# Score steps of four blocks instead of two or three, in an attention and long-convolution kernel

## The chip, the cores and the metric

The kernel runs on one core of a Trainium2 chip. The core has five engines, each with its own instruction queue, that meet only in semaphores: TensorE (PE, matmuls, with its weight loads PEld), VectorE (DVE), ScalarE (ACT), GpSimd (POOL) and SyncE (SP); the last two mostly start DMAs here. Matmuls write to PSUM, which has eight banks of 128 partitions x 512 fp32. The metric is the device time of one execution in microseconds (us), the median over runs.

## The reference

Two independent computations write the two halves of the output.

```python
# A: multi-head attention, S = 2048, D = 512, 32 heads of 16
qkv = (x @ wqkv) split into q, k, v by head
p = softmax(q k^T * 16**-0.5)          # 32 x 2048 x 2048
a = (p @ v, heads joined) @ wo
# B: gated long convolution, 512 channels
kv = (4-tap causal filter of k, by channel) * v
y  = causal convolution of kv with ssm_k along S, by channel   (there by FFT)
b  = q * (y + kv * ssm_D)
out = concatenate([a, b])
```

The 32 x 2048 x 2048 exponentials of A are the largest item: 2048 blocks of 128 keys x 512 queries.

## The kernel before

**Blocks and groups.** A *group* is one of 32: four heads (of the eight that share 128 rows of a projection, every second) and 512 queries. It has 64 *blocks*, 16 key tiles of 128 times 4 heads, and the head of a block decides which 32 rows of the PE array its score matmul takes (`tile_position=(32 * s, 0)`); matmuls in different row groups run side by side. The blocks go through in order in a queue, in *steps* T = 0, 1, 2, ...

**A step.** `emit_qk` takes the step's PSUM banks and as many blocks, `qk_mm` issues their scores (L803). One block of a step may go to VectorE, the others are made into exponentials by one ScalarE instruction over neighbouring banks (`emit_exp`, L836) that writes the ring PT (17 blocks). On VectorE a block takes four operations (`exp_on_dve`): the first reads the bank (L882), and three work in SBUF on the ring PTD (8 blocks): L888, L892, L896. They give two halves, both of which are multiplied by V. `emit_pv` multiplies exponentials by V (L933), four heads side by side in four column groups, into bank 6 (PVB), over the whole group; two steps after the scores at the earliest. When a group is complete, `finish_group` transposes bank 6 on VectorE (L1007) and normalises (L1014, L1018, and for every second group L1027).

**Banks.** Banks 0 to 5 are for scores; even steps take them from the left, odd ones from the right, up to `MOST` = 3 a step, so that a step's banks are read while the next step's are written. `take_banks` moves the border as banks come free and may let the last bank come late (`late`). Bank 7 (BGB) collects the convolution.

**Background work on TensorE.** *Units* are the projections q, k, v, the 4-tap filter kv, the output projection op and the transposes of a finished piece of convolution ("turn"). Ahead of step `N_OPEN` = 64 they use bank 7. Later each needs a *window*: `hold` takes one score bank out of circulation for `LEN` = 3 steps, and `unit_step` puts units into it in halves. In the meantime no block goes to VectorE where a unit is close. The convolution (`conv_lags`, L1143) runs in bank 7 in portions between the other work. `warm_up` fills gaps with matmuls on zeros (L1353).

**What sets the order.** All orders are written out when the program is built. A planner (`Eng.op`) keeps a running time for each engine, adds a duration to each operation, and the rules (`room`, `unit_step`, `advance`, `pv_step`) decide by these times what to issue next. VectorE's later operations stand in `flow` and are let in by `advance`; `urgent` puts an operation in at once. Each engine then runs its list in order, with semaphore waits. For every 256 words of TensorE's code three DMA loads of filter rows (`feed_wr`) are released.

**The end.** The last 2 x `N_TAIL` = 18 blocks go in nine steps of two, without VectorE, while the output projection of the last queries fills in.

Of the kernel before, what the change touches and what calls it, by code (L numbers as in the profile page):

```python
# [34 lines left out]
R_PT = 17  # L35
# [5 lines left out]
N_OPEN = 64  # L41
KV1 = 3
LAGS = 8
PACE = 1.2
# [16 lines left out]
N_TAIL = 9  # L61
N_LAST = 0
# [3 lines left out]
R_PTD = 8  # L66
T_DVE = 6
SLOT = 18
OPEN = 80
CLOSE = 10  # L70
REST = 4
LEN = 3
WIN_D = 2
# [4 lines left out]
PLAN = 710  # L78
JOIN = 0.1
JOIN2 = 0.15  # L80
MOST = 3
Q_DUE = 24
LOOK = 8
GAP = 7
TAIL_GAP = 0
AHEAD = 6
KZ_LATE = 8.0
KEEP = 4
BACKLOG = 6.0
# [7 lines left out]
TURN = 0.05  # L97
SOON = 0.5
NEAR = 0.1
FULL = 1.6  # L100
BUSY = 0.85
FILL_GAP = 0.2
RATE = 4.2
CAP = 18.0
WAIT = 3
# [147 lines left out]
def bass_concat_heads__mha_block__ssm_conv_h3__prompt_kernel(  # L253
# [47 lines left out]
    DR = sb("DR", [128, NQB * NG, 16], FP32)  # L301
# [175 lines left out]
    def pe_unit(u, bank, parts=(0, 1, 2, 3)):  # L477
# [3 lines left out]
        if kind == "q":  # L481
# [3 lines left out]
            def mm(e, dc):  # L485
                return e.matmul(PS[:, bank, :], lhsT=WQ[:, dc, o * 128:(o + 1) * 128], rhs=xT[:, dc, qb * 512:(qb + 1) * 512],  # L486
                                start=(dc == 0), stop=(dc == 3))
        elif kind == "k":
# [5 lines left out]
            def mm(e, dc):  # L494
                return e.matmul(PS[:, bank, c0:512], lhsT=WK[:, dc, o * 128:(o + 1) * 128],  # L495
                                rhs=xT[:, dc, sc * 512 + c0:(sc + 1) * 512], start=(dc == 0), stop=(dc == 3))
        elif kind == "kv":
# [5 lines left out]
            def mm(e, b):  # L503
                ins = None
                for m in range(4):
                    c0 = LEFT + 128 * (4 * i + 3 - b) - m
                    ins = e.matmul(PS[:, bank, 128 * b:128 * b + 128], lhsT=KTR[kt_i][:, kt_c, c0:c0 + 128], rhs=DG[:, c, m, :],
                                   start=(m == 0), stop=(m == 3))
                return ins
        else:  # L510
# [10 lines left out]

        def fn(e):
            ins = None
            for j in parts:
                ins = mm(e, j)
            return ins
        return pe.op(fn, deps, run=mm_run * len(parts), kind="F")
# [133 lines left out]
    ends = [4, 4]  # L661
    LAST_BLKS = 2 * N_TAIL + 3 * N_LAST
    NL = NQB * NG - 1
    held = {}
    win = {}
    queue = list(range(NBLK))

    def take_banks(T):
        if len(queue) == LAST_BLKS:
            end[0] = T + N_TAIL + N_LAST  # L670
        if len(queue) <= LAST_BLKS:
            return [3 * (T % 2) + i for i in range(2 + (len(queue) > 2 * N_TAIL))]
        start = max(pe.t, at(h_exp.get(T - 2)) + 0.13)
        late["bank"] = None

        def comes_free(b):
            if held.get(b) == "w" and (part[0] or T <= win["stop"] and (T < win["begin"] + 2 or near(T, CLOSE))):
                return False
            if at(bank_free[b]) + 0.13 > start + JOIN and late["bank"] is None and T >= 2:
                if at(bank_free[b]) + 0.13 + JOIN2 <= at(h_exp[T - 1]) - 0.36:  # L680
                    late["bank"] = b
            return at(bank_free[b]) + 0.13 <= start + JOIN or late["bank"] == b

        def give(b):
            if held.pop(b, None) == "w":
                win.clear()
                win["last"] = T
        if T % 2 == 0:
            while ends[0] < min(ends[1], MOST) and comes_free(ends[0]):
                give(ends[0])  # L690
                ends[0] += 1
            banks = list(range(ends[0]))
        else:
            while ends[1] > max(ends[0], 6 - MOST) and comes_free(ends[1] - 1):
                give(ends[1] - 1)
                ends[1] -= 1
            banks = list(range(ends[1], 6))
        if T >= N_OPEN and near(T, OPEN) and T >= win.get("last", 0) + REST and "bank" not in win and len(banks) > 2 and late["bank"] is None and len(queue) > LAST_BLKS + OPEN_LAST:
            b = hold(T, banks, "w")
            win.clear()  # L700
            win.update(bank=b, begin=T, stop=T + LEN)
        return banks

    def near(T, most):
        job = next_unit(T)
        return job is not None and job[0] - T <= most

    def hold(T, banks, kind):
        if T % 2 == 0:
            b = banks.pop()  # L710
            ends[0] -= 1
        else:
            b = banks.pop(0)
            ends[1] += 1
        held[b] = kind
        h_held[b] = T
        return b

    end = [10 ** 6]
    h_held = {}  # L720
    late = {"bank": None}
# [28 lines left out]
    h_blk = {}  # L750
    def emit_qk(T):
        banks = take_banks(T)
        n = min(len(banks), len(queue) - LAST_BLKS) if len(queue) > LAST_BLKS else len(banks)
        bl = next_blocks(n)
        extra = dve_block(T, bl) if late["bank"] is None else None
        d_bank = hold(T, banks, "d") if extra is not None else None
        if extra is not None:
            if extra not in bl:
                bl.pop()
                bl.append(extra)  # L760
            n -= 1
        banks = banks[:n]
        for b in bl:
            queue.remove(b)
        banks_of[T] = banks
        chunks[T] = bl
        for b in bl:
            chunk_of[b] = T
        on = list(zip(bl, banks + [d_bank]))
        if late["bank"] in banks and len(queue) >= LAST_BLKS:  # L770
            i = banks.index(late["bank"])
            h = qk_mm(on[:i] + on[i + 1:])
            emit_exp(T, bl, banks, h, extra, d_bank, [on[i]])
        else:
            h = qk_mm(on)
            emit_exp(T, bl, banks, h, extra, d_bank, [])

    def next_blocks(n):
        bl = []
        for b in [b for b in queue[:LOOK] if blk_group(b) == blk_group(queue[0])] + queue[:n]:  # L780
            if len(bl) < n and b not in bl and (blk(b)[2] not in [blk(x)[2] for x in bl] or len(bl) + 1 > 4):
                bl.append(b)
        for b in queue[:n]:
            if len(bl) < n and b not in bl:
                bl.append(b)
        return bl
# [30 lines left out]
    def emit_exp(T, bl, banks, h, extra, d_bank, more):  # L817
        n = len(banks)
        if extra is not None:
            on_dve[extra] = len(on_dve)  # L820
            exp_on_dve(extra, d_bank, h)
# [4 lines left out]
        for i, b in enumerate(bl[:n]):  # L826
            assert p0 + i not in pt_used
            pt_used[p0 + i] = b
            pt_of[b] = p0 + i
        if more:  # L830
            if at(bank_free[more[0][1]]) + 0.13 > pe.t + 0.1:
                advance(pe.t)
                pv_step(T)
            h = qk_mm(more)
        free = max([pt_free[p] for p in range(p0, p0 + n) if p in pt_free], key=lambda d: d[1], default=None)
        h_exp[T] = act.op(lambda e: e.activation(PT[:, p0:p0 + n, :].rearrange("p b f -> p (b f)"),  # L836
                                                 PS[:, banks[0]:banks[0] + n, :].rearrange("p b f -> p (b f)"),
                                                 ACT.Exp, scale=EXP_SCALE, bias=EXP_BIAS),
                          [h, free], us=(0.065 + 0.4257 * n, 0.205 + 0.4257 * n))
        for b, bank in zip(bl[:n], banks):  # L840
            bank_free[bank] = h_blk[b] = h_exp[T]
# [8 lines left out]
    def dve_block(T, bl):  # L850
        if len(bl) < 3 or WIN_D and "bank" in win and (part[0] or WIN_D > 1 and near(T, CLOSE)) or T < T_DVE or len(queue) < LAST_BLKS + 3 * (TAIL_GAP - N_LAST) + 3:
            return None
        i = len(on_dve)
        if i >= R_PTD and i - R_PTD not in h_ptd:
            return None
        todo = sum(us[0] for f in flow for _, _, _, us, _ in f)
        if max(dve.t - pe.t, 0.0) + todo > BACKLOG:
            return None
        n, j = sub(bl[-1])
        left = len([b for b in queue if sub(b) == (n, j)])  # L860
        if left - 3 >= 2.6 * GAP:
            return bl[-1]
        if n == NL:
            if (n, j + 1) not in [sub(b) for b in queue]:
                return None
            ahead = [b for b in queue if sub(b) == (n, j + 1)]
        else:
            n += 1
            ahead = [b for b in queue if blk_group(b) == n]
            if len(ahead) < 4 * KT - AHEAD + 1 or n not in h_q or (OF[n], 0) not in h_k:  # L870
                return None
        rows = [blk(b)[2] for b in bl[:-1]]
        return next((b for b in ahead[:4] if blk(b)[2] not in rows), ahead[0])
# [84 lines left out]

    acts, dves = [], []
# [6 lines left out]
    def pv_step(T):  # L966
# [519 lines left out]
```

## Time and profile before

| | before |
|---|---|
| median of 3 runs | 784.3 us (781.27 to 792.7) |
| the profiled execution | 787.65 us, its span 785.9 us |
| granted TensorE clock, mean | 0.978 |
| ScalarE busy | 754.8 us |
| TensorE busy | 736.5 us |
| VectorE busy | 686.0 us |
| GpSimd busy | 90.7 us |

All rows and views are of one profiled execution; its time is 3.35 us over the median. A row of the grouping view names line, engine, operation, what is written and read, the shape and the count, then busy time and mean length of one (ns), then the idle time ahead of these instructions and what ended it. A row of the timeline has the start, the length, and in brackets the idle time of the engine before it with what ended it. Instructions of an engine overlap a little, so their lengths add up to more than the busy time, and the time that one takes in a chain is read from starts.

### The profile page before, as it was taken

The numbers are of one execution on the slowest core, as the hardware profiler recorded it, in microseconds if no ns is written. First come the engines' busy times: TensorE is split into PE (matmuls) and PEld (weight loads), VectorE is DVE, ScalarE is ACT, GpSimd is POOL, SyncE is SP. The second block draws the span as 40 slices with busy tenths as digits, with TensorE's granted clock in tenths as the row PEclk, the third lists the DMA queues.
The fourth block names the chain that finished last, engine by engine and source line by source line (L and its number), as shares of the span: only waits on it lengthen the run. The fifth ranks groups of instructions, "written<-read, shape, count | busy, mean of one in ns | idle before, by whom it ended". The sixth has DMA issues, their size and how long they took to land.

```text
span 785.9 us, 31776 instructions
## 1 busy us (share of the span) xinstructions
PE 736.5 (94%) x14087; PEld 319.2 (41%) x14132; DVE 686.0 (87%) x1887; ACT 754.8 (96%) x735; POOL 90.7 (12%) x160
## 2 busy tenths in 40 slices
PE   8999998998989999999999999999999999999987
PEld 3233443443424344344443334443443434434453
DVE  4999777899989999898798889989999978889992
ACT  6999999999979999999999999999999999999994
POOL 6300102200400201000022020004011010000000
PEclk9999999999979999999999999999999999999995
DMA  9895149858546576667865766857686775767510
GB/s 221 217 287 175 36 155 238 288 168 266 175 169 217 195 235 210 220 231 212 260 201 181 233 210 215 258 185 245 211 275 185 222 250 178 256 236 224 193 57 28
DMA packets 88888, 161.45 MB, mean 205 GB/s; under 512 B 50256, under 2 KB 53968, under 8 KB 88368
## 3 DMA queue, kind: packets, MB, share of 16 engines
q1 hardware_dynamic: 81760, 150.43, 60.7%
q0 software_dynamic: 5792, 8.66, 3.6%
q8 instruction: 112, 1.84, 1.0%
q10 hardware_dynamic: 1200, 0.33, 0.2%
q14 instruction: 24, 0.20, 0.1%
HBM read 142.61 MB, written 6.42 MB: 190 GB/s over the span
## 4 chain that ended last, share of the span: by engine, by line
ACT 60%; DVE 22%; PE 17%; issue 1%; DMA 1%
ACT PT L836 60%; DVE PTD L882 9%; PE PS L803 6%; PE PS L933 5%; DVE PTD L892 4%; DVE PTD L888 3%; DVE PTD L896 2%; PE PS L1143 2%; PE PS L1081 2%; DVE DT L1007 1%; DMA xT<-in_A_x_dram 1%; PE PS L486 1%; DVE QN L1176 1%; DVE KTo L543 0%; DVE VA L571 0%
## 5 line engine op out<-in xcount | busy, mean ns | idle before, releaser
L836 ACT ACTIVATE PT<-PS 128x1024 bf16<-128x1024 f32 (+2 forms) x731 | 752.6, 1251 | 19.3 <-PE PS L803 18.0
L803 PE MATMUL PS<-QT,KTo 32*128 32x512 bf16 (+2 forms) x2248 | 292.5, 370 | 22.6 <-ACT PT L836 9.5
L882 DVE TENSOR_SCALAR PTD<-PS 128x512 uint16<-128x512 f32 x406 | 276.1, 684 | 35.6 <-PE PS L803 34.3
L933 PE MATMUL PS<-PT,VA 128*32 128x512 bf16 (+2 forms) x1800 | 207.2, 377 | 11.8 <-DVE DT L1007 7.5
L1143 PE MATMUL PS<-WR,KV 128*28 128x128 bf16 (+8 forms) x8192 | 199.4, 220 | 0.0
L1143 PEld LDWEIGHTS PS<-WR,KV 128*28 128x28 bf16 (+7 forms) x8192 | 143.9, 95 | 63.9 <-issue 34.4
L892 DVE TENSOR_TENSOR PTD<-PTD 128x512 f16<-128x512 f16 x406 | 163.4, 417 | 1.3
L803 PEld LDWEIGHTS PS<-QT,KTo 32*128 32x128 bf16 x2248 | 76.1, 92 | 206.0 <-ACT PT L836 150.2
L933 PE MATMUL PS<-PTD,VA 128*32 128x512 f16 (+1 forms) x896 | 149.2, 370 | 1.2 <-DVE PTD L896 1.2
L896 DVE TENSOR_SCALAR PTD<-PTD 128x512 uint16<-128x512 uint16 x406 | 111.0, 286 | 0.9
L888 DVE TENSOR_SCALAR PTD<-PTD 128x512 uint16<-128x512 uint16 x406 | 109.7, 290 | 1.3
L348 POOL DMA_DIRECT2D QT<-QS x120 | 61.0, 516 | 414.7 <-DVE QS L534 369.0
L933 PEld LDWEIGHTS PS<-PT,VA 128*32 128x32 bf16 x1800 | 52.8, 95 | 124.5 <-issue 90.2
L1353 PE MATMUL PS<-IDN,ZW 128*32 128x512 bf16 (+3 forms) x197 | 51.6, 317 | 0.1
L933 PEld LDWEIGHTS PS<-PTD,VA 128*32 128x32 bf16 x896 | 37.3, 96 | 5.6 <-DVE PTD L896 1.7
L1007 DVE STREAM_TRANSPOSE DT<-PS 128x512 f32<-128x512 f32 x31 | 22.1, 713 | 5.9 <-PE PS L933 5.3
L1089 DVE CAST OUTA<-PS 128x512 bf16<-128x512 f32 x15 | 10.3, 687 | 12.5 <-PE PS L1081 12.2
L348 POOL DMA_DIRECT2D out_dram<-OUTA x15 | 8.7, 582 | 108.0 <-DVE OUTA L1089 34.1
L1353 PEld LDWEIGHTS PS<-IDN,ZW 128*32 128x32 bf16 x197 | 16.3, 97 | 11.1 <-issue 5.8
L1081 PE MATMUL PS<-WKV,OTN 128*128 128x512 bf16 (+1 forms) x54 | 18.8, 422 | 2.1 <-issue 0.8
L543 DVE CAST KTo<-PS 128x512 bf16<-128x512 f32 (+1 forms) x16 | 10.7, 670 | 10.1 <-PE PS L495 10.1
L518 PE MATMUL PS<-WKV,xT 128*128 128x128 bf16 x256 | 19.3, 220 | 0.0
(71 smaller groups left out, 232.7 us busy)
## 6 DMA issues: line engine op xcount, KB each, us to landing
WR<-kz_scratch SPq DMA_DIRECT2D x256, 512.0 KB, 5.9
KV<-KV SPq DMA_DIRECT2D x16, 256.0 KB, 5.4
kz_scratch<-WR SPq DMA_DIRECT2D x1, 2176.0 KB, 9.4
QN<-in_B_q_dram POOLq DMA_DIRECT2D x2, 1024.0 KB, 10.1
out_dram<-QN POOLq DMA_DIRECT2D x2, 1024.0 KB, 6.5
QT<-QS POOLq DMA_DIRECT2D x120, 16.0 KB, 3.5
out_dram<-OUTA POOLq DMA_DIRECT2D x15, 128.0 KB, 2.9
QN<-in_B_ssm_k_dram SPq DMA_DIRECT2D x1, 1024.0 KB, 8.5
```

The lines of the kernel that those rows point to most:

```text
L348: f(outp, inp).then_inc(dsem.sem, 16)
L803: ins = e.matmul(PS[:, bank, i * w:i * w + w], lhsT=KTo[32 * s:32 * s + 32, OF[n_] % 2, kt * 128:(kt + 1) * 128], rhs=QT[32 * s:32 * s + 3 ...
L836: h_exp[T] = act.op(lambda e: e.activation(PT[:, p0:p0 + n, :].rearrange("p b f -> p (b f)"), PS[:, banks[0]:banks[0] + n, :].rearrange("p ...
L882: h_f = urgent(lambda e: e.tensor_scalar(fix_u, PS[:, bank, :], FIX_ADD, FIX_HI, ALU.add, ALU.min), [h, h_ptd.get(i - R_PTD)], slack=S_FX)
L888: st["h"] = dve.op(lambda e: e.tensor_scalar(mant_u, fix_u, MANT, HALF_BITS, ALU.bitwise_and, ALU.bitwise_or), [st["h"]], us=us)
L892: st["h"] = dve.op(lambda e: e.tensor_tensor(mant, fix, mant, ALU.mult), [st["h"]], us=us)
L896: lambda e: e.tensor_scalar(fix_u, fix_u, OCTAVE, ONE_MORE, ALU.bitwise_and, ALU.bitwise_or), [st["h"]], us=us)
L933: ins = e.matmul(dst, lhsT=w, rhs=rhs, start=first, stop=last, tile_position=(0, 32 * s))
L1007: h_t = urgent(lambda e: e.transpose(out=dt, in_=PS[:, PVB, :]), [h, h_mul.get(n - 1)], slack=S_T, us=(0.63, 0.751))
L1081: ins = e.matmul(PS[:, b, c0:c1], lhsT=OTN[:, PAIRS.index((o, qb)), t * 128:(t + 1) * 128], rhs=WO[:, o, c0:c1], start=(o == 0), stop=(o = ...
L1143: ins = e.matmul(PS[32 * g:32 * g + 2 * ((30 - d) // 2 + 1), BGB, 128 * kk:128 * kk + w], lhsT=kv, rhs=WR[:, r + g, S - 64 * d - 128:S - 6 ...
L1353: pe.op(lambda e, s=s, k=k, rhs=rhs, bank=bank, rows=rows, c0=c0, first=first: e.matmul(PS[32 * s:32 * s + rows, bank, c0:c0 + 128 * k], l ...
```

## The change

Steps have four blocks, with one block in each row group. Bank 4 and the pair 0-1 or 2-3 (in turns) go to ScalarE in two instructions, first one block, then two; bank 5 goes to VectorE. Where VectorE gets no block, ScalarE does two pairs, (4, 5) and then (0, 1) or (2, 3). So banks 4 and 5 are used by every step. Windows are gone: units use bank 7 between pieces of the convolution, in quarters, and q, k and op matmuls of 128 columns are cut into four of 32 columns in four column groups (`columns`), as P times V has them.

```diff
-R_PT = 17
+R_PT = 15
...
-N_OPEN = 64
...
+N_OPEN = 50
...
-N_TAIL = 9
...
+N_TAIL = 10
...
-R_PTD = 8
...
+R_PTD = 10
+DV_MIN = 4
+LOOK = 16
+LAST_PV = 5
...
-BACKLOG = 6.0
+BACKLOG = 4.0
...
-    DR = sb("DR", [128, NQB * NG, 16], FP32)
+    DR = sb("DR", [128, 2, 16], FP32)
...
+    def columns(e, dst, w, rhs, **kw):
+        ins = None
+        for g in range(0, 128, 32):
+            ins = e.matmul(dst[g:g + 32], lhsT=w[:, g:g + 32], rhs=rhs, tile_position=(0, g), **kw)
+        return ins
...
+            return [2 * (T % 2) + i for i in range(2)]
+        return step_banks(T)
+
+    def step_banks(T):
+        return [4, 2 * (T % 2), 2 * (T % 2) + 1, 5]
...
+    def next_blocks(T):
+        main = queue[:min(LOOK, len(queue) - LAST_BLKS)]
+        d = dve_block(T, main)
+        bl = []
+        for b in main:
+            if b != d and len(bl) < 4 - (d is not None) and blk(b)[2] not in [blk(x)[2] for x in bl + [d] if x is not None]:
+                bl.append(b)
...
+        return bl + [d] * (d is not None), d
+
     def emit_qk(T):
         banks = take_banks(T)
...
+        bl, extra = next_blocks(T) if len(banks) == 4 else (queue[:2], None)
         for b in bl:
             queue.remove(b)
...
             chunk_of[b] = T
...
+        if len(bl) == 4 and extra is None:
+            banks = [4, 5, banks[1], banks[2]]
+        banks_of[T], chunks[T] = banks[:4 - (extra is not None)] if len(bl) == 4 else banks, bl
+        h = qk_mm(list(zip(bl, banks)))
+        if extra is not None:
+            on_dve[extra] = len(on_dve)
+            exp_on_dve(extra, banks[3], h)
+        n = len(bl) - (extra is not None)
+        for i, j in ((0, n - 2), (n - 2, n)) if n > 2 else ((0, n),):
+            h_exp[T] = emit_exp(bl[i:j], banks[i:j], h)
...
+    def dve_block(T, main):
+        i = len(on_dve)
+        if T < T_DVE or i >= R_PTD and i - R_PTD not in h_ptd or backlog() > BACKLOG:
             return None
...
             close = all(i in chunk_of for i in own) and T >= max(chunk_of[i] for i in own) + 2
-            if close:
+            late = close and (T >= max(chunk_of[i] for i in own) + LAST_PV or n == NL or force)
+            if late:
                 for b, part in d:
                     while b not in h_blk:
...
+    def at_rest():
+        return not state["lag"] and state["qd"] % 4 == 0 and not any(pv_n.get((NL, i, 128)) for i in range(4))
...
             if u[0] == "turn":
+                if free + pe.turn("F") + 0.223 + SWITCH > lim + 0.05:
+                    return
                 conv_turn(u[1], bank)
                 state["turn"] = False
                 continue
...
+            n = min(4 - k, int((room + over) / one))
+            if n < 1:
+                return
...
+            h = pe_unit(u, bank, range(k, k + n))
```

`at_rest` is true when no piece of the convolution is open in bank 7; only then do units run, and only when no unit is due does the convolution go on. `pv_make_room` forces P times V where the smaller ring PT has no room. The filter-row loads keep their rate of three for 256 words of code, now carried over in fractions.

The written order changes throughout. On ScalarE, 554 exponentials of two blocks, 174 of three and 3 of four become 564 of two and 460 of one. On VectorE, 406 blocks become 460. On TensorE, the matmuls on zeros grow from 197 to 467, and all instructions together from 14,135 to 14,972.

TensorE in the middle of the convolution, before: L803 are scores, L1143 convolution, L933 P times V (of PT from ScalarE, of PTD from VectorE), `s_dve` and `s_act` the semaphores of VectorE and ScalarE.

```order
L803 MATMUL PS<-QT,KTo 128x512 [waits s_dve,s_act]
L803 MATMUL PS<-QT,KTo 128x512 x2
L1143 MATMUL PS<-WR,KV 22x128 x8
L1143 MATMUL PS<-WR,KV 20x128 x8
L1143 MATMUL PS<-WR,KV 18x128 x8
L1143 MATMUL PS<-WR,KV 16x128 x8
L803 MATMUL PS<-QT,KTo 128x512 [waits s_dve,s_act]
L803 MATMUL PS<-QT,KTo 128x512 x2
L933 MATMUL PS<-PT,VA 32x512 x4
```

The same kind of place now: L756 are scores, L869 P times V, L1105 convolution and L1311 matmuls on zeros.

```order
L756 MATMUL PS<-QT,KTo 128x512 [waits s_act,s_dve]
L756 MATMUL PS<-QT,KTo 128x512 x3
L869 MATMUL PS<-PT,VA 32x512 x3
L869 MATMUL PS<-PTD,VA 32x512
L1105 MATMUL PS<-WR,KV 30x128 x8
L1105 MATMUL PS<-WR,KV 28x128 x8
L1105 MATMUL PS<-WR,KV 26x128 x4
L1311 MATMUL PS<-IDN,ZW 32x512
L756 MATMUL PS<-QT,KTo 128x512 [waits s_dve,s_act]
L756 MATMUL PS<-QT,KTo 128x512 x3
```

A group of scores has four matmuls instead of three, and it waits for VectorE and ScalarE: for bank 5, which the step before gave to VectorE, and for bank 4.

VectorE in the middle of the convolution, before: L882 is a block's first operation, which reads its bank, L888, L892 and L896 the later three.

```order
L882 TENSOR_SCALAR PTD<-PS 128x512
L888 TENSOR_SCALAR PTD<-PTD 128x512 x2
L882 TENSOR_SCALAR PTD<-PS 128x512
L892 TENSOR_TENSOR PTD<-PTD 128x512
L882 TENSOR_SCALAR PTD<-PS 128x512
L896 TENSOR_SCALAR PTD<-PTD 128x512
```

And now: L818 is the first operation, L824, L828 and L832 the later three; L1120 empties the convolution's bank, L1138 multiplies a transposed piece by q, L541 takes a projected q.

```order
L818 TENSOR_SCALAR PTD<-PS 128x512
L1120 CAST YB<-PS 128x512
L818 TENSOR_SCALAR PTD<-PS 128x512
L1138 TENSOR_TENSOR QN<-PS,QN 128x16x2x16
L818 TENSOR_SCALAR PTD<-PS 128x512
L832 TENSOR_SCALAR PTD<-PTD 128x512
L828 TENSOR_TENSOR PTD<-PTD 128x512
L824 TENSOR_SCALAR PTD<-PTD 128x512
L818 TENSOR_SCALAR PTD<-PS 128x512
L832 TENSOR_SCALAR PTD<-PTD 128x512
L541 TENSOR_SCALAR QS<-PS 128x512
```

Between two first operations stand, instead of one later operation, either the three later ones of a block or one that reads another bank.

374 lines of the change are left out of this document (143 added, 231 removed).

## The prediction

> **What bounds the kernel now.** I read the page first, for the share of each engine and for the chain that ended last.
>
> ```profile
> span 785.9 us, 31776 instructions
> PE 736.5 (94%) x14087; PEld 319.2 (41%) x14132; DVE 686.0 (87%) x1887; ACT 754.8 (96%) x735; POOL 90.7 (12%) x160
> ...
> ACT 60%; DVE 22%; PE 17%; issue 1%; DMA 1%
> ...
> L836 ACT ACTIVATE PT<-PS 128x1024 bf16<-128x1024 f32 (+2 forms) x731 | 752.6, 1251 | 19.3 <-PE PS L803 18.0
> ```
>
> ScalarE is the bound: its 731 exponentials fill 752.6 of 785.9 us, and the chain runs over it for 60%. What it loses between them is 19.3 us, of which 18.0 us are waits for scores (L803). The timeline of ScalarE tells where these waits are, and that of TensorE and two stretches of busy time tell what stood before the larger ones.
>
> ```profile
> 137.23 0.40 PE L933 MATMUL PS<-PTD,VA 128*32 128x512 f16 x4 [0.88 <-DVE PTD L896]
> 138.00 3.28 ACT L836 ACTIVATE PT<-PS 128x1024 bf16<-128x1024 f32 x3 [1.58 <-PE PS L803]
> 190.84 0.45 PE L933 MATMUL PS<-PT,VA 128*32 128x512 bf16 x3 [1.04 <-DVE PTD L896]
> 226.29 0.61 PE L1169 MATMUL PS<-IDN,YB 128*128 128x128 bf16 x4 [1.64 <-DVE YB L1158]
> 778.26 1.02 ACT L836 ACTIVATE PT<-PS 128x1024 bf16<-128x1024 f32 x1 [0.48 <-PE PS L803]
> ...
> 186.00:198.00 12.00, 10.07 (x183) 3.68 (x182) 11.33 (x35) 10.46 (x12) 0.00 (x0) 0.86 0.85 312
> 224.00:242.00 18.00, 15.81 (x238) 5.70 (x231) 12.72 (x34) 12.80 (x13) 0.00 (x0) 0.62 0.24 81
> ```
>
> The last columns of a stretch are PE, PEld, DVE, ACT and POOL busy, granted clock, DMA share and GB/s. Three times TensorE stood still for VectorE (0.88, 1.04 and 1.64 us), and after the last two the granted clock was 0.86 and 0.62 in the stretch, in which ScalarE lost 12 - 10.46 = 1.5 and 18 - 12.80 = 5.2 us. With the 1.58 us at 138 these are 8.3 us. The eight steps at the end lose about 0.5 us each, as the row at 778.26 does, some 4.5 us. About 5 us of the 18.0 are scattered.
>
> **ScalarE's own work.** What one instruction costs in a chain is read from starts.
>
> ```profile
> 7.97 2.79 ACT L836 ACTIVATE PT<-PS 128x2048 bf16<-128x2048 f32 x2 [0.50 <-PE PS L803]
> 9.74 9.57 ACT L836 ACTIVATE PT<-PS 128x1024 bf16<-128x1024 f32 x8
> 227.71 1.45 ACT L836 ACTIVATE PT<-PS 128x1536 bf16<-128x1536 f32 x1 [1.23 <-PE PS L803]
> 229.75 1.02 ACT L836 ACTIVATE PT<-PS 128x1024 bf16<-128x1024 f32 x1 [0.59 <-PE PS L803]
> 757.79 2.85 ACT L836 ACTIVATE PT<-PS 128x1024 bf16<-128x1024 f32 x3 [0.19 <-PE PS L803]
> ...
> L836 ACT ACTIVATE PT<-PS 128x1024 bf16<-128x1024 f32 x554 | 540.4, 1148 | 15.7 <-PE PS L803 15.0
> L836 ACT ACTIVATE PT<-PS 128x1536 bf16<-128x1536 f32 x174 | 262.4, 1565 | 3.0 <-PE PS L803 2.5
> ```
>
> Four blocks take 9.74 - 7.97 = 1.77 us from start to start. Of three instructions of two blocks the last is 1.02 long, so each takes (2.85 - 1.02) / 2 = 0.915. A block is then (1.77 - 0.915) / 2 = 0.4275 us and the fixed part 0.06; three blocks are 1.3425, and one block, a form that the trace lacks, is 0.4875. Before there are 554 of two, 174 of three and 3 of four: 506.9 + 233.6 + 5.3 = 745.8 us. The new order has 564 of two and 460 of one: 516.1 + 224.3 = 740.4. 54 blocks fewer save 23 us, and 293 more fixed parts take 17.6 of it back: **-5.5 us**.
>
> [...]
>
> **VectorE.** Its share goes from 406 to 460 blocks, 54 x (0.60 + 0.20 + 0.33 + 0.20) = 72 us more work, with these durations taken from one start to the next.
>
> ```profile
> 404.23 0.29 DVE L888 TENSOR_SCALAR PTD<-PTD 128x512 uint16<-128x512 uint16 x1
> 404.43 0.68 DVE L882 TENSOR_SCALAR PTD<-PS 128x512 uint16<-128x512 f32 x1
> 405.03 0.42 DVE L892 TENSOR_TENSOR PTD<-PTD 128x512 f16<-128x512 f16 x1
> 405.37 0.68 DVE L882 TENSOR_SCALAR PTD<-PS 128x512 uint16<-128x512 f32 x1
> 405.97 0.28 DVE L896 TENSOR_SCALAR PTD<-PTD 128x512 uint16<-128x512 uint16 x1
> 406.17 0.69 DVE L882 TENSOR_SCALAR PTD<-PS 128x512 uint16<-128x512 f32 x1
> ...
> L1007 DVE STREAM_TRANSPOSE DT<-PS 128x512 f32<-128x512 f32 x31 | 22.1, 713 | 5.9 <-PE PS L933 5.3
> L571 DVE CAST VA<-PS 128x512 bf16<-128x512 f32 x16 | 11.0, 688 | 3.5 <-PE PS L518 3.5
> L1014 DVE RECIPROCAL DR<-DT 128x16 f32<-128x16 f32 x31 | 7.4, 239 | 0.1
> L1018 DVE TENSOR_TENSOR DTN<-DT,DR 128x256 bf16<-128x256 f32 x31 | 12.9, 416 | 0.2
> ```
>
> An instruction that lasts 0.68 lets the next start after 0.60, so I take 0.08 off each mean: a transpose 0.63, any read of a whole bank 0.60, a reciprocal 0.16, a product of 256 columns 0.33. I price every row of the new VectorE order so and add it up between one block's first operation and the next one's. The 460 pieces sum to 726 us, and ScalarE's instructions between the same points (0.4875 + 0.915 = 1.40 a step, and 1.83 more for a step without a VectorE block) to 735. VectorE, 87% busy before, has only 9 us left, with the two engines in step.
>
> What the lack of slack costs hangs on the banks. A group of scores needs all four banks; bank 4 was read by the ScalarE instruction just before, bank 5 by VectorE, and neither has a twin. In the new TensorE order 461 of 518 groups of scores wait for both engines.
>
> ```profile
> 402.07 0.39 PE L803 MATMUL PS<-QT,KTo 32*128 32x512 bf16 x3
> 402.39 0.40 PE L933 MATMUL PS<-PT,VA 128*32 128x512 bf16 x4
> 402.58 0.68 DVE L882 TENSOR_SCALAR PTD<-PS 128x512 uint16<-128x512 f32 x1
> ```
>
> The loop over VectorE is 0.39 (scores), 0.12 (402.46 to 402.58) and 0.68: 1.19 us, under 1.40. The loop over ScalarE is 1.02 - 0.43 = 0.59 for the single block and 0.39: scores stand ready up to 1.40 - 0.98 = 0.4 us early, less a hop of 0.12 on each side, 0.2. 177 of the 460 pieces hold just one block's four operations, 1.33 us. 166 are longer than ScalarE's part, by 30.4 us in all. If VectorE's lag is carried on, worked off by the shorter pieces, and costs ScalarE only what exceeds the allowance, it costs 4.9 us at 0.4, 10.6 at 0.2 and 30.4 at nothing. A gain is excluded, since the sum for ScalarE holds no wait. I take the middle one, **+10.6 us**.
>
> **TensorE.** Four blocks of scores lie in four row groups. Four matmuls in four column groups took 0.40 (402.39), three in row groups 0.39, so the fourth costs nothing; at worst one more pass, as a matmul's 0.2. Groups of scores fall from 731 to 518, and the projections in 32-column pieces cost what the row at 402.39 shows, as much as a whole one. What is freed goes to matmuls on zeros, 197 before and 467 now. None of this is on the path while ScalarE's 1.40 us a step cover it: with P times V and convolution a step holds 0.39 + 0.40 + about 0.4. Without that cover each excess is added as it is.
>
> Two of the old causes change. A finished head's P times V, which stood before the waits at 137 and 190 (L896), may now stay open for up to five steps, and the transposes of the convolution, before the wait at 226 (L1158), go in only when the bank they read from is free. I take those three waits with what followed out: **-8.3 us**; ends 0 and -13 (with all scattered ones). The smaller ring of exponentials (15 for 17) holds five steps, and P times V runs two behind: nothing, unless that lag grows to five. The DMAs are the same in number (256 loads of filter rows), a load being tied to code blocks of TensorE as before. The end has ten steps of two blocks for nine: **+0.5 us**.
>
> **The sum** is made against the profiled execution, 787.65 us (span 785.9 and 1.75 around it), which is 3.35 over the median of 784.3: 787.65 - 5.5 + 10.6 - 8.3 + 0.5 = 784.95; less 3.35, **782 us**. That is no change: a measurement of this kernel tells about 2% from none, 768.6 to 800.0.
>
> **Rivals.** *VectorE sets the pace (slower).* Place: bank 5, from a block's first operation to the next scores. If the allowance is used up by hops and late starts, all 30.4 us come through, and the three old waits stay in another guise: 787.65 - 5.5 + 0.5 + 30.4 = 813.0, less 3.35 is 810. It decides from waits of 21 us. For it speaks that VectorE itself waits for TensorE, and that in the new order such an operation stands between two first operations:
>
> ```profile
> DVE OUTA L1089 <- PE PS L1081: 12.2, 7, 4.1
> DVE KTo L543 <- PE PS L495: 10.1, 6, 3.0
> DVE KV L556 <- PE PS L507: 8.0, 6, 2.4
> ```
>
> Against it, these waits fell where VectorE had nothing queued. [...] Chance 0.17.
>
> *TensorE's clock falls more often.* The stretch 224 to 242 cost 5.2 us after one wait of 1.64 us. TensorE now waits at almost every step, if briefly. Six such stretches: 787.65 - 5.5 + 4.9 - 8.3 + 0.5 + 31 = 810, less 3.35 is 807. Against it: 467 matmuls on zeros. Chance 0.07.
>
> *Everything is absorbed (faster).* The lag costs 1 us and all 13 us of waits ahead of the end go: 787.65 - 5.5 + 0.5 + 1 - 13 = 770.65, less 3.35 is 767. Chance 0.13.
>
> *The single block pays the fixed part that an instruction alone has.* 1.02 - 2 x 0.43 = 0.16 instead of 0.06: 460 x 0.1 = 46 us, 828. The chain of 0.915 speaks against it. Chance 0.03.
>
> That the change does not do what it says is excluded as to counts, which the order shows.
>
> **Numbers.** The forecast has 0.60. Faster by over 2% is the absorbed case, 0.13; slower the pace, the clock and the fixed part, 0.27. The range, 767 to 810, reaches to the absorbed case and the pace; about half of each lies beyond, with the fixed part, some 0.2 in all. The forecast's own range is 776 (lag at 4.9) to 790 (old waits kept).
>
> **What would show it.** Right: exponentials of one block at 0.49 us from start to start, busy ScalarE near 747 us, VectorE over 95% busy between 30 and 750 us, ScalarE's waits for scores near 20 us in many pieces of 0.1 to 0.4 us, no stretch of half clock ahead of the end. Wrong: waits of scores for VectorE's first operation on most steps (the pace), a granted clock under 0.9 in several stretches, or a step of over 1.45 us with no wait on ScalarE. What would make it wrong above all is the allowance: I worked it out from rows in which each bank had a twin.

## The result and the profile after

| | before | after |
|---|---|---|
| median | 785.96 us (781.27 to 792.7, 4 runs) | 821.12 us (818.11 to 830.01, 4 runs) |
| ratio, 95% interval | | 1.046, 1.035 to 1.057 |
| profiled execution, its span | 787.65, 785.9 us | 821.45, 819.7 us |
| granted TensorE clock, mean | 0.978 | 0.968 |
| ScalarE waits for scores | 18.0 us, 33 | 53.1 us, 47 |
| matmuls held up for at least 0.9 us by nothing that the profile names | none | 14, 30.4 us |

The change made the kernel 4.6% slower; 821 lies outside the range that was given. Some executions of two kernels below (experiments 6 and 7) were over 1.5% longer than the fastest of the same kernel; they are left out of their medians and ratios. The page of the changed kernel, its span, the busy times, the chain that ended last, the queue that brings code, and the dearest groups on ScalarE and VectorE:

```profile
span 819.7 us, 34068 instructions
PE 721.5 (88%) x14969; PEld 343.0 (42%) x14969; DVE 743.2 (91%) x2103; ACT 753.0 (92%) x1028; POOL 92.7 (11%) x160
...
q8 instruction: 119, 1.95, 1.0%
...
DVE 45%; ACT 29%; PE 18%; issue 5%; DMA 2%
...
L783 ACT ACTIVATE PT<-PS 128x1024 bf16<-128x1024 f32 (+1 forms) x1024 | 750.7, 915 | 54.7 <-PE PS L756 53.1
L818 DVE TENSOR_SCALAR PTD<-PS 128x512 uint16<-128x512 f32 x460 | 312.8, 680 | 43.0 <-PE PS L756 42.1
```

ScalarE's work shrank a little (752.6 to 750.7 us), but it and VectorE both wait for TensorE's scores, 53.1 and 42.1 us. TensorE, the engine that both wait for, is itself idle more than before (88% busy for 94%). The view of waits gives for each pair the sum, the count and the longest, in us. In the changed kernel:

```profile
ACT PT L783 <- PE PS L756: 53.1, 47, 3.9
...
PE PS L756 <- DVE PTD L818: 17.9, 63, 1.1
...
PE PS L1105 <- issue: 14.3, 7, 3.5
PE PS L756 <- issue: 13.5, 9, 3.8
...
PE PS L869 <- issue: 7.1, 8, 1.9
```

"Issue" means that no semaphore held the instruction back. Before, the longest such wait of a score or convolution matmul was 0.5 us:

```profile
PE PS L803 <- issue: 0.5, 1, 0.5
```

The timeline of the changed kernel around the longest one (start, length, and in brackets the idle time before):

```profile
478.70 0.39 PE L756 MATMUL PS<-QT,KTo 32*128 32x512 bf16 x3
...
482.86 0.09 PEld L756 LDWEIGHTS PS<-QT,KTo 32*128 32x128 bf16 x1 [4.06 <-issue]
482.86 0.38 PE L756 MATMUL PS<-QT,KTo 32*128 32x512 bf16 x1 [3.76 <-issue]
...
483.28 1.51 ACT L783 ACTIVATE PT<-PS 128x512 bf16<-128x512 f32 x2 [3.91 <-PE PS L756]
483.29 0.69 DVE L818 TENSOR_SCALAR PTD<-PS 128x512 uint16<-128x512 f32 x1 [3.94 <-PE PS L756]
```

Three of four score matmuls of one group ran, the fourth came 3.76 us later, with its weight load. Nothing in the program stands between them. ScalarE and VectorE wait 3.9 us for that one matmul.

**The stops stand on code borders.** Counting two code words for a matmul (its weight load and itself) and one for every semaphore instruction in the trace, from the planner's start of 65 words on, each of the 14 stops falls within two words of a multiple of 256. Queue q8 moved 119 packets of 16 KB, and TensorE's code has 119 such blocks (112 and 112 before): each packet is one block. In the view of the DMA queues (packets, MB, share) the packet of the block in question can be found; first the 7 us from the border before it, then the next half us:

```profile
DMA packets 599, 2.18 MB, mean 311 GB/s; under 512 B 68, under 2 KB 68, under 8 KB 599
...
q1 hardware_dynamic: 599, 2.18, 97.0%
...
WR<-kz_scratch SPq DMA_DIRECT2D x3, 512.0 KB, 7.0
```

```profile
DMA packets 37, 0.15 MB, mean 303 GB/s; under 512 B 3, under 2 KB 3, under 8 KB 36
...
q1 hardware_dynamic: 36, 0.14, 65.9%
q8 instruction: 1, 0.02, 12.0%
```

TensorE entered a block at 473.4 us. From 473.5 to 480.5 the filter rows (queue q1) kept the DMA engines 97% busy and no code came; the packet started at 480.7, 7.3 us behind the border. TensorE had reached the end of its block at 478.7 and went on at 482.86, 2.2 us behind the start of the packet and 1.2 us behind its end. All 14 stops end 2.2 to 2.5 us behind the start of a packet, and these packets started 3.2 to 7.3 us behind their borders.

I placed every packet (by its start) and every border (the first matmul of a block, by counting words) in six of the traces. Behind the first 20 blocks, this is the delay of a packet behind its border, and how close the borders are:

```
kernel                       packets  mean us  4 us or more  latest  next border     third border    stops
                                                                     within 4.5 us   within 15 us
before                          92      1.3        2          4.7         9               2            0
before, larger doses            92      1.4        3          4.2        12               1            0
after                           99      2.3       19          7.3        20              21           14
after, rows cut to 1/16         99      1.5        3          4.4        28              27            0
after, smaller doses            99      2.4       15          7.7        31              20           12
after, borders held apart       98      2.4       22          7.7        19              11            9
```

The second row and the last three are experiments below. In the changed kernel borders follow closer on each other, since all convolution now runs between the phases of units, and a code block often comes late. With the rows cut the borders are closer still, yet only 3 packets are 4 us late or more and nothing stops for 0.9 us: in that trace near borders alone did not stop TensorE, and with the 19 late packets of the changed kernel there were 14 stops.

**What follows a stop.** The stretches around the first stop (2.50 us, ending at 157.27) have PE, PEld, DVE, ACT and POOL busy, then granted clock, DMA share and GB/s:

```profile
154.00:157.00 3.00, 0.77 (x27) 0.38 (x18) 0.99 (x4) 1.04 (x2) 0.00 (x0) 0.87 0.17 67
158.00:163.00 5.00, 5.00 (x76) 2.23 (x69) 3.97 (x9) 3.58 (x5) 0.00 (x0) 0.50 0.69 193
163.00:166.00 3.00, 2.94 (x38) 1.44 (x36) 2.93 (x7) 3.00 (x5) 0.00 (x0) 0.99 0.59 209
```

After the stop TensorE runs at half clock (0.50 granted) for 5 us, and ScalarE loses 5 - 3.58 = 1.42 us more. The trace has 11 stretches of half clock ahead of the end, of 3.4 or 6.8 us. Nine belong to stops. The other two, at 456.6 and 528.3 us, stand behind shorter waits: TensorE had waited for VectorE and ScalarE, step after step and up to 0.73 us at a time, ahead of the first, and 0.90 us for ScalarE, then 0.73 us by issue, ahead of the second. ScalarE lost 3.2 and 0.9 us there.

### The profile page after: what moved, and what is told of

The parts are those of the page before. It is cut to its first block, busy times and chain, and to the rows that moved or that the text cites. A ratio compares the mean times of both kernels' runs of the same rounds, so it can differ in the third digit from the quotient of the medians.

```text
span 819.7 us, 34068 instructions
## 1 busy us (share of the span) xinstructions
PE 721.5 (88%) x14969; PEld 343.0 (42%) x14969; DVE 743.2 (91%) x2103; ACT 753.0 (92%) x1028; POOL 92.7 (11%) x160
## 4 chain that ended last, share of the span: by engine, by line
DVE 45%; ACT 29%; PE 18%; issue 5%; DMA 2%
ACT PT L783 29%; DVE PTD L818 18%; DVE PTD L828 9%; PE PS L756 6%; DVE PTD L824 6%; DVE PTD L832 5%; PE PS L1105 5%; PE PS L869 5%; DVE DT L959 1%; PE PS L1311 1%; DMA QN<-in_B_k_dram 1%; DVE KV L563 1%; DVE QN L1138 1%; DVE QS L541 1%; DVE YB L1120 1%
## 5 line engine op out<-in xcount | busy, mean ns | idle before, releaser
L783 ACT ACTIVATE PT<-PS 128x1024 bf16<-128x1024 f32 (+1 forms) x1024 | 750.7, 915 | 54.7 <-PE PS L756 53.1
L818 DVE TENSOR_SCALAR PTD<-PS 128x512 uint16<-128x512 f32 x460 | 312.8, 680 | 43.0 <-PE PS L756 42.1
L756 PE MATMUL PS<-QT,KTo 32*128 32x512 bf16 (+2 forms) x2248 | 215.4, 373 | 58.8 <-DVE PTD L818 17.9
L869 PE MATMUL PS<-PT,VA 128*32 128x512 bf16 (+2 forms) x1755 | 202.1, 376 | 8.8 <-issue 4.3
L869 PE MATMUL PS<-PTD,VA 128*32 128x512 f16 (+1 forms) x986 | 194.5, 381 | 4.0 <-issue 2.9
L1105 PE MATMUL PS<-WR,KV 128*28 128x128 bf16 (+9 forms) x8192 | 184.7, 224 | 14.3 <-issue 14.3
L828 DVE TENSOR_TENSOR PTD<-PTD 128x512 f16<-128x512 f16 x460 | 185.4, 410 | 0.4
L1105 PEld LDWEIGHTS PS<-WR,KV 128*30 128x30 bf16 (+8 forms) x8192 | 153.9, 96 | 51.7 <-issue 22.5
L756 PEld LDWEIGHTS PS<-QT,KTo 32*128 32x128 bf16 x2248 | 62.3, 91 | 194.7 <-ACT PT L783 105.5
L832 DVE TENSOR_SCALAR PTD<-PTD 128x512 uint16<-128x512 uint16 x460 | 126.1, 277 | 0.1
L824 DVE TENSOR_SCALAR PTD<-PTD 128x512 uint16<-128x512 uint16 x460 | 122.8, 282 | 0.1
L1311 PE MATMUL PS<-IDN,ZW 128*32 128x512 bf16 (+3 forms) x467 | 112.5, 329 | 0.0
L869 PEld LDWEIGHTS PS<-PT,VA 128*32 128x32 bf16 x1755 | 50.0, 94 | 116.4 <-issue 95.2
L1311 PEld LDWEIGHTS PS<-IDN,ZW 128*32 128x32 bf16 x467 | 42.0, 98 | 32.1 <-issue 3.4
L869 PEld LDWEIGHTS PS<-PTD,VA 128*32 128x32 bf16 x986 | 45.0, 95 | 12.9 <-issue 8.9
L1120 DVE CAST YB<-PS 128x512 bf16<-128x512 f32 x16 | 11.0, 689 | 5.7 <-PE PS L1105 5.4
```

The costliest lines, as they stand in the source:

```text
L756: ins = e.matmul(PS[:, bank, i * w:i * w + w], lhsT=KTo[32 * s:32 * s + 32, OF[n_] % 2, kt * 128:(kt + 1) * 128], rhs=QT[32 * s:32 * s + 3 ...
L783: h = act.op(lambda e: e.activation(PT[:, p0:p0 + n, :], src, ACT.Exp, scale=EXP_SCALE, bias=EXP_BIAS), [h, free], us=(0.065 + 0.4257 * n, ...
L818: h_f = urgent(lambda e: e.tensor_scalar(fix_u, PS[:, bank, :], FIX_ADD, FIX_HI, ALU.add, ALU.min), [h, h_ptd.get(i - R_PTD)], slack=S_FX)
L824: st["h"] = dve.op(lambda e: e.tensor_scalar(mant_u, fix_u, MANT, HALF_BITS, ALU.bitwise_and, ALU.bitwise_or), [st["h"]], us=us)
L828: st["h"] = dve.op(lambda e: e.tensor_tensor(mant, fix, mant, ALU.mult), [st["h"]], us=us)
L832: lambda e: e.tensor_scalar(fix_u, fix_u, OCTAVE, ONE_MORE, ALU.bitwise_and, ALU.bitwise_or), [st["h"]], us=us)
```

## The experiments

All numbers of ScalarE's waits are those for scores; "stops" are matmuls held up for at least 0.9 us by issue. Ratios are to the kernel before, timed beside it.

**1. Rows cut to 1/16.** The loads of filter rows behind the first ring bring 128 of 2048 columns; the number, order and waits of the loads and all of TensorE's code stay. The convolution then multiplies old columns.

```diff
-            src = bass.AP(tensor=kz_ap.tensor, offset=kz_ap[row, 0].offset, ap=[[1, 64], [64 * LKZ, 2], [1, S]])
-            h_wr[qd] = dma(sp, d_wr[i], WR[:, 4 * i + g, :], src, [h_kzw[0], dep, h], kb=512, rate=WR_KB, late=2.95)
+            cols = S if qd < R_W // 4 else 128
+            src = bass.AP(tensor=kz_ap.tensor, offset=kz_ap[row, 0].offset, ap=[[1, 64], [64 * LKZ, 2], [1, cols]])
+            h_wr[qd] = dma(sp, d_wr[i], WR[:, 4 * i + g, 0:cols], src, [h_kzw[0], dep, h], kb=512, rate=WR_KB, late=2.95)
```

> The changed kernel, but each load of filter rows after the first three sets brings 128 of its 2048 columns (the convolution is then computed from stale rows); order and waits of all engines are the same. Theory C (TensorE stops at borders of 256 words of its code because the next 16 KB of code come behind the filter rows in the DMA engines): the stops of over 0.9 us that end in issue, 14 of them with 30 us before, fall to 3 or fewer, and the time to 780 to 792. Theory P (VectorE sets the pace through bank 5, the slower rival): 812 or more, and VectorE's part of the chain of waits stays over 40%.

Measured: 774.42 us, ratio 0.984 (0.978 to 0.991); no stops, ScalarE waits 9.2 us. The same program with less data in flight is 47 us faster than the changed kernel, and faster than theory C had it (780 to 792). VectorE's pace, theory P, is not what costs them, though the chain that ended last runs over VectorE for 66%.

**2. Half of the rows' columns.** 1024 in place of 128 in the same line.

> As the kernel with 128 columns, but each of these loads brings 1024 of 2048 columns, half the bytes. Theory C: between the two, if the DMA engines' backlog is what the code waits for, nearer to the kernel without them, 785 to 800, with at most 5 stops. Theory P: 812 or more.

Measured: 788.13 us (one run), 5 stops, 9.5 us; waits 22.9 us. Stops and time go with the bytes: 0, 9.5, 30.4 us for 1/16, half and all columns.

**3. A shorter VectorE block.** The operation L832 on 16 of its 512 columns, which leaves part of the exponentials unfinished.

```diff
-                lambda e: e.tensor_scalar(fix_u, fix_u, OCTAVE, ONE_MORE, ALU.bitwise_and, ALU.bitwise_or), [st["h"]], us=us)
+                lambda e: e.tensor_scalar(fix_u[:, 0:16], fix_u[:, 0:16], OCTAVE, ONE_MORE, ALU.bitwise_and, ALU.bitwise_or), [st["h"]], us=us)
```

> The changed kernel, but the last of VectorE's four operations of a block is done on 16 of 512 columns (part of the exponentials is then wrong); order and waits are the same. That frees about 0.13 x 460 = 60 us of VectorE. Theory P: the time falls by 25 us or more, under 797. Theory C: the stops stay, and the time falls by less than 12 us, to 809 to 821.

Measured: 820.17 us (one run), 17 stops, 38.5 us. VectorE's busy time fell from 743.2 to 712.0 us, 0.07 us a block and half of the 60 us that were expected, and the time stayed: VectorE's pace is not on the path while the stops are there.

**4. The kernel before with the new doses of convolution.**

```diff
-LAGS = 8
-PACE = 1.2
+LAGS = 14
+PACE = 2
...
-RATE = 4.2
-CAP = 18.0
+RATE = 7
+CAP = 30
```

> The kernel before, with the convolution let out in the bursts of the changed one (up to 14 lags a step for 8, and the rate, its cap and the pace that go with it), its steps and banks unchanged. Theory C: code is used up in bursts here too, stops of over 0.9 us at borders of code appear (none before), and the time rises by 8 to 40 us, to 794 to 826. Theory P: within 1% of before.

Measured: 780.25 us (5 runs), ratio 0.992 (0.987 to 0.997); no stops. Theory C failed; the time is within theory P's 1%. The four numbers alone do not bring the borders together: the third border is within 15 us once, before twice, after the change 21 times. The old three waits are gone instead, in the page of this kernel:

```profile
span 777.9 us, 31828 instructions
...
L836 ACT ACTIVATE PT<-PS 128x1024 bf16<-128x1024 f32 (+2 forms) x730 | 754.9, 1230 | 6.0 <-PE PS L803 4.9
```

So the larger dose alone is not the cause; it takes the new frame (steps of 1.4 us, units and convolution in turns). And this version is 0.8% faster than the kernel before.

**5. Smaller doses in the changed kernel.**

```diff
-LAGS = 14
+LAGS = 10
...
-RATE = 7
+RATE = 5
```

> The changed kernel with its two numbers for the convolution's dose lowered: at most 10 lags a step in place of 14, and 5 in place of 7 in its rate. The 256 loads of filter rows stay whole. Theory C (late code: borders of 256 code words come every 4 to 5 us in the dense steps, each lets 1.5 MB of filter rows go, and the next code block waits behind them): with 10 lags a step the borders stand further apart, so the stops of TensorE fall from 14 to at most 7, their sum from 30 us to 15 or less, and the time to 788 to 808 us. Theory R (the stops come from the number of code words that the steps of four need, wherever the convolution stands): 10 or more stops, and 812 us or more.

Measured: 799.85 us, ratio 1.011 (1.008 to 1.014), 12 stops, 21.6 us, waits 32.3 us. The time is as theory C had it. The sum of the stops is over its 15 us, and their number is as theory R had it, but they are shorter (1.8 us a stop for 2.2). The borders do not stand further apart, as theory C would have them (20 third borders within 15 us for 21), and packets of 4 us or more are 15 for 19; what makes the stops shorter is not shown.

**6. Rows let go one at a time.**

```diff
-    due_wr = [0.0]
+    due_wr = [0.0, 0.0]
...
-        due_wr[0] = min(due_wr[0] + GATE, GATE + 1)
-        feed_wr(int(due_wr[0]), h)
-        due_wr[0] -= int(due_wr[0])
+        due_wr[0] += GATE
...
+        if due_wr[0] >= 1 and pe.t >= due_wr[1] + 1.0:
+            feed_wr(1, (pe.sem, pe.n))
+            due_wr[0] -= 1
+            due_wr[1] = pe.t
```

> The changed kernel with the same 256 whole loads of filter rows in the same order, but let go one at a time, at least 1 us of planned time apart, in place of three together at each border of a code block. Theory C, if it is the burst of 1.5 MB just at the border that holds the next code block up: stops fall to at most 7 and the time to 785 to 805 us. Its rival B (not the burst, but the mean demand of the dense stretches, which one load each us, 0.5 MB, fills as well): 10 or more stops again, 810 us or more.

Measured: 810.4 us (806.94 and 813.79), ratio 1.025 (1.019 to 1.031), 18 stops, 28.4 us. Rival B holds by the stops and, barely, by the time: it is not the burst of three loads at the border alone. That the loads of one border are not done when the next block of code is asked for fits, but is not shown by this.

**7. The planner's charge doubled.** `NEED` from 8 to 16.

> The changed kernel with the planner's charge for a convolution lag that would reach the next code block before it has landed, doubled from 8 to 16 a us. Theory C with the reason in the order (the planner lets the convolution run into blocks that are still on their way): stops at most 9, 795 to 812 us. If the planner's own landing times are too early, the charge changes nothing: 12 or more stops, 815 us or more.

Measured: 808.1 us (800.87 to 809.33, 3 runs), ratio 1.020 (1.014 to 1.026). The profiled execution, with 17 stops of 34.2 us, took 814.74 us, more than these three. Its stops fit the other case, that the planner's landing times are too early; the time is within what theory C had. So this run decides nothing.

**8. The control: the kernel before with its rows cut to 1/16.** The edit of experiment 1, here once a slot of the ring has been filled.

> The kernel before with the later loads of filter rows cut to 128 of 2048 columns (the products of those lags are then made from old columns). It is the control to the same edit of the changed kernel, which took 774.4 us. Theory C: the kernel before has no stops to lose, so it gains little, 775 to 787 us, and beside it the steps of four alone bring 0 to 12 us. Theory G (the row loads slow both kernels in some other way, such as through the memory that engines share with them): it gains as the changed one did, below 770 us, and the steps of four alone bring nothing or lose.

Measured: 789.02 us (10 runs), ratio 0.998 (0.994 to 1.002). That is no change, 2 us above what theory C had. The kernel before loses nothing to its row loads, so experiment 1 does not gain from cheaper loads as such; theory G falls.

**9 and 10. Borders held apart.** The planner takes a code block to land not before 9 us after the border two before it and 15 us after the third before it, with 16 lags a step and with 14.

```diff
+        self.crosses = [-99.0, -99.0]
...
-        return max(cross + FETCH, end + LOADED)
+        self.crosses.append(cross)
+        return max(cross + FETCH, end + LOADED, self.crosses[-2] + 9, self.crosses[-3] + 15)
```

> The changed kernel with one more rule in the planner: it holds convolution back so that a code block of TensorE is not entered before 9 us after the border two before it and 15 us after the border three before it, and up to 16 lags a step where it may run. All 256 loads of filter rows stay whole, three let go at each border as in the changed kernel. In the changed kernel the measured stops stand mostly behind the second or third border within 13 us. Theory C with this as the point (short series of borders, not the amount of code or rows): stops fall from 14 to at most 5 and their sum from 30 us to 10 or less, time 776 to 796 us. Theory R (amount): 10 or more stops, 805 us or more. If the held convolution only comes too late elsewhere, stops vanish and the time stays above 800 us.

> The same rule for the borders with 14 lags a step as in the changed kernel, so that the rule is the only difference to it. Theory C: at most 6 stops, 12 us or less in all, time 778 to 798 us. Theory R: 10 or more stops, 805 us or more.

Measured with 16: 806.91 us, 1.025 (1.020 to 1.031), 9 stops, 15.2 us. With 14, so with the rule as the only difference to the changed kernel: 799.62 us (791.47 to 801.97), 1.013 (1.007 to 1.019), 9 stops, 14.1 us. Its waits:

```profile
ACT PT L785 <- PE PS L758: 27.3, 34, 2.2
...
PE PS L1107 <- issue: 12.0, 9, 2.4
...
PE PS L871 <- issue: 4.1, 6, 1.9
...
PE PS L758 <- issue: 1.9, 3, 1.4
```

The rule halves the stops' sum and takes 21 us off, but not all, and both theories missed the count; theory C missed the times as well, by 10.9 and 1.6 us. By the table above its packets are as late as in the changed kernel (22 by 4 us or more for 19), and as many borders are within 4.5 us of the one before; but series of borders are half as many (the third within 15 us 11 times for 21). So it fits that series of borders decide what late packets cost, and experiments 1 and 2 show that the row loads decide how late most of them are.

**11 and 12. What VectorE's pace costs without stops.** Experiments 1 and 3 together (the shortened operation is the fourth of a block, the third behind the one that reads the bank), and experiment 1 again beside it.

> Both edits at once: the later filter rows cut to 128 of 2048 columns, and the third operation of a VectorE block (the one that keeps the octave bits) on 16 of its 512 columns, some 0.2 us less of VectorE in each of 460 steps. Without the stops of TensorE this shows what VectorE's pace costs. Theory V (the prediction's term: what VectorE lags behind ScalarE's 1.4 us a step is on the path, 10.6 us): 8 to 12 us under the same kernel with the whole operation, 762 to 767 us. Theory N (VectorE's lag is made up in the one-block exponentials and at the ends, and ScalarE ends last anyway): within 4 us of it, 770 to 776 us.

> The changed kernel with the later filter rows cut to 128 of 2048 columns and nothing else, timed again beside the run above: 772 to 777 us by either theory, as it took 774.4 us before, with no stop of TensorE.

Measured: 769.06 us (6 runs), ratio 0.977 (0.972 to 0.981), and 773.91 us (6 runs), 0.983 (0.977 to 0.988). The shorter block takes 31.7 us off VectorE's busy time (741.5 to 709.8), 0.07 us in a block and not the 0.2 that was expected, and gains 4.9 us, between the two theories. The pages, first with the whole operation, then with the short one (span, chain, ScalarE's exponentials):

```profile
span 773.0 us, 34060 instructions
...
DVE 71%; ACT 15%; PE 11%; DMA 2%; issue 1%
...
L783 ACT ACTIVATE PT<-PS 128x1024 bf16<-128x1024 f32 (+1 forms) x1024 | 746.8, 926 | 12.9 <-PE PS L756 11.6
```

```profile
span 766.6 us, 34060 instructions
...
ACT 86%; DVE 6%; PE 6%; DMA 2%; issue 1%
...
L783 ACT ACTIVATE PT<-PS 128x1024 bf16<-128x1024 f32 (+1 forms) x1024 | 744.4, 1028 | 7.6 <-PE PS L756 7.5
```

A chain that runs 71% over VectorE gave 4.9 us for 31.7 us of VectorE's time: with the short operation it passes to ScalarE, whose own chain is only 773.0 - 766.6 = 6.4 us shorter. One stop, of 1.0 us, is left in the trace with the whole operation, and none with the short one.

## Why the prediction was wrong

**The step that failed** is the one on TensorE: "None of this is on the path while ScalarE's 1.40 us a step cover it", with "The DMAs are the same in number (256 loads of filter rows), a load being tied to code blocks of TensorE as before" put at nothing. The number of loads, their size and their rate per code block did stay. What changed is when code blocks come: the convolution, eight lags a step beside everything else before, now runs in phases of up to 14 lags in 1.4 us steps, and between them stand the units. Borders of 256 words then come in series, while 1.5 MB of rows for each border are still under way, and the next block of code comes late. No engine's row priced this, because before the change it cost nothing: no stop, and the latest packet of 92 started 4.7 us behind its border. The trace of before did have the queue of code (112 packets) and a DMA share of 0.5 to 0.8 in most slices, and the planner of both kernels has a term for code that is still on its way (`fetch`, with `FETCH` = 3.3 us behind the border at least). How far behind each border the packet started, and how close the borders would stand in the new order, could have been worked out from these.

By profiled executions, this is the whole loss. Against experiment 12 the changed kernel's span is 819.7 - 773.0 = 46.7 us longer, of which ScalarE's waits are 53.1 - 11.6 = 41.5 and its busy time 750.7 - 746.8 = 3.9. The stops themselves are 30.4 us of it; the rest of the 41.5 us of waits fits what follows them at half clock. In the trace of the changed kernel 30.6 us of ScalarE's idle time stand around the stops and 13.9 us in and just behind the stretches of half clock, of which 4.1 in the two that no such stop precedes.

**The other terms**, against experiments 11 and 12, where the stops are away:
- *ScalarE's own work, -5.5.* Right: 746.8 for 752.6, -5.8 us. The one-block form, which the trace lacked, costs what was worked out for it, and the fixed part that an instruction alone has (rival, 828) did not come.
- *VectorE's lag, +10.6.* The sign is right: taking 31.7 us of VectorE's work away gained 4.9 us. That this is also the prediction's lower end, at an allowance of 0.4 us, is chance: the operation was shortened by 0.07 us a block, not by the whole lag, so 4.9 us is what the lag costs at least.
- *The old waits, -8.3, and the end, +0.5.* With the short VectorE operation ScalarE's waits fell from 18.0 to 7.5, by 10.5 us. 4.5 us of these are the end: before, its nine exponentials took 13.7 us with 4.5 us of waits, at half clock from 764.5 us on; in experiments 11 and 12, and in the changed kernel, ten take 9.7 us without a wait. The prediction kept these waits and added 0.5. The 6.0 us that are left are less than the 8.3. The reason that it gave for the 8.3 is not shown: in experiment 4 ScalarE's waits fall to 4.9 us by the larger doses alone, with the old way of P times V and transposes.
- *Net.* The sum was -2.7 us on the kernel before; without the stops the medians are 14.3 us apart (773.9 against 788.2), the profiled spans 12.9 (773.0 against 785.9). Of the 10.2 us between -2.7 and -12.9, 5.7 are VectorE's lag and 5.0 the end, while the old waits go the other way by 2.3; some 2 us are not assigned. The change holds the larger doses too, which alone gained 0.8% in experiment 4; how much of the 1.7% here is owed to the steps of four themselves was not tried apart.

**The rivals.** The fixed part of the single block (828) was nearest in time, and ScalarE's busy time excludes it. "VectorE sets the pace" (810) has a reason that experiment 3 excludes. "TensorE's clock falls more often" (807) saw the half clock, which came in 11 stretches ahead of the end, but nine of them with stops that no rival had; its own mechanism, many short waits, shows at 456.6 us, where ScalarE lost 3.2 us. "Everything is absorbed" (767) is close to what the steps of four do when code arrives in time.

**What was to show it.** Exponentials of one block were to take 0.49 us from start to start and do (0.48). VectorE was to be over 95% busy between 30 and 750 us and is 93% (668.6 of 720 us). ScalarE's waits were to be near 20 us in pieces of 0.1 to 0.4; they are 53.1 in 47 pieces of up to 3.9. The list of signs of a wrong forecast had waits for VectorE and a low clock, not a matmul that waits for nothing.

**What stays open.** Why some blocks are late even where few bytes move: from the 18th block on, nine packets of experiment 1 start 3.3 to 4.4 us behind their border, with the DMA engines 8 to 14% busy, and at just these nine the changed kernel, with the same code, is 5.2 to 7.3 us late and stops. So the bytes of the rows account for 1.3 to 3.2 us of the delay there, and no run shows what the rest comes from; the number of loads and of their packets is the same in both. Which part of the new frame brings the borders together (the steps, the quarters, or that units and convolution exclude each other) was not tried apart, nor a larger ring of filter rows, which would let loads run through the phases of units.

## What to carry to other kernels

When an order gets denser in one place, count what each engine must be fed there, its own code too: here every 256 words of TensorE's code need a 16 KB packet that shares the DMA engines with the data, and a change that kept the loads' totals made it late (4 us or more behind its border for 2 of 92 packets before and 19 of 99 after). A matmul that waits for "issue" in the middle of a group was the sign (all 14 waits of at least 0.9 us stood at such borders); look for its place in the code and for the code queue's packet. A chain that runs mostly over one engine doesn't say what that engine is worth: shorten it and see (here 31.7 us less work on the engine with 71% of the chain gave 4.9 us).

## What the runs showed of the hardware

- TensorE went on 1.2 to 1.6 us behind the end of a code packet in all 102 stops of at least 0.9 us, in nine of the traces (changed kernel and experiments 2, 3, 5 to 7, 9, 10 and 12). From the packet's start it was 2.2 to 3.3 us, and 2.2 to 2.5 us in the 14 stops of the changed kernel.
- The longer such a stop, the more often half clock came with it, during the stop or up to 2 us behind it: at none of 29 stops of 0.9 to 1.3 us, 2 of 10 of 1.3 to 1.5, 24 of 43 of 1.5 to 2.5, and 19 of 20 of 2.5 us and more. In the changed kernel it was nine of the ten of at least 1.5 us. The shortest stop with half clock was 1.57 us in the changed kernel and 1.32 us in experiment 6.
